# Masked numerators of the first 18 chunks read the scores in PSUM, with a new order for the first third of the work

## The chip, the cores and the metric

The kernel runs on one core of one Trainium2 chip. The metric is the device time of one execution in microseconds (us), as the median of several runs. Before the change it is 442.39 us, from 3 runs between 442.03 and 442.68 us.

Names of engines, as the profile has them: PE is TensorE (PEld is its weight load), DVE is VectorE, ACT is ScalarE, POOL is GpSimd, SP is SyncE, which here only issues DMAs.

## The reference, cut to what matters

Attention with a threshold, for 8 batches of 8 heads with 576 rows and 64 columns each, and then a feed-forward layer with a maximum of three products:

```python
scores = scale * np.matmul(q, k.transpose(0, 1, 3, 2))
thresh = np.max(scores, axis=-1, keepdims=True) - tau
scores = np.where(scores >= thresh, scores, -1000000000.0)
scores = scores - np.max(scores, axis=-1, keepdims=True)
attn = np.exp(scores)
attn = attn / (np.sum(attn, axis=-1, keepdims=True) + 1e-09)
attn_out = np.matmul(attn, v)
...
h = np.maximum(np.maximum(x @ w1, x @ w2), x @ w3)
return h @ w_out
```

Here x is attn_out with heads and columns side by side: 4608 rows of 512. A row keeps only the scores within tau = 0.02 of its largest one; the others become zero in the softmax.

## The kernel before, in words

**Tiles.** The heads of a batch come in two groups of four, called quads (16 quads, g = 0 to 15). A quad has 9 chunks (idx), and a chunk has two tiles (r = 0 and 1). A tile is 128 rows of queries by 576 keys in float32, made by `scores` (line 286) in one of four PSUM slots, s0 to s3, of two banks each (`bank`, line 182). There are 144 chunks and 288 tiles. The first 18 chunks are batch 0, quads 0 and 1.

**The path of one tile.** `maximum` (line 318) reads the scores on DVE and gives a statistic of each row for the bias of the next step: the negated maximum for a masked tile, the maximum less tau for a plain one. `exponents` (line 330) runs on ACT. `numerators` (line 338) gives the numerators of the softmax and their sum. Each tile goes one of two ways, by a digit of the string MASKED (line 24, two digits to a chunk; `masked`, line 310):

- Digit 1, a masked tile. `maximum` writes the negated scores to the SBUF tile z, and its accumulator gives their minimum. After that the PSUM slot is free. `exponents` takes Exp of z in place. `numerators` on DVE (letter k) multiplies z by the test z >= exp(-tau).
- Digit 0, a plain tile. `maximum` writes a bfloat16 tile `unused` that nobody reads, for the accumulator alone. `exponents` reads the scores in PSUM with Prelu, which writes z; then the slot is free. `numerators` on ACT (letter n) takes Exp of z with a factor that sends what lies below the threshold to zero. It issues a second, short ACT instruction that reads the accumulator.

In the first 18 chunks (g < 2) the numerators go straight to P in bfloat16, and their sums are applied later to the product with v (`spread`, line 356, letters R, D, b). For the other chunks they stay in z, and DVE's `reciprocals` (letter r) and POOL's `normalized` (letter p) make P. Then `turned` (line 381, letter t) issues a DMA transpose of the chunk's P on SP.

**After the tiles.** `product` (line 387) multiplies the transposed P with v (letter O, with N for the ninth chunk), and DVE or ACT takes the result out (w and x). `ffn` (line 461) runs the three hidden products (F and B) of a batch, with their evacuation on ACT (h) and DVE (v), and the output products (u, stores o). The hidden products of batch 0 need all four products of quads 0 and 1, so they need all 18 transposes.

**The order.** Every engine works strictly in order: the class `_Ordered` (line 82) ties each instruction to the one before it on its engine. The order of all of them is the string ORDER (line 40), read letter by letter by the loop at line 757 and `issue` (line 634). A digit behind S, T, O, F or D is the PSUM slot that it uses. The letters by engine:

- PE: S scores, T transposes of q and k (`transposed`, line 255), O, N, F, B, D
- DVE: m maximum, k masked numerators, c copy of k, v, w, r, R
- ACT: e exponents, n plain numerators, a copy of q, b, h, x, u
- POOL: q, p, y, z
- SP: l loads of q, k, v (`load`, line 186), g weight loads, t transposes, o stores

All instructions go through one helper, so the profile puts them all down to L91; a tile's name tells them apart (sc: scores in PSUM, z, P, nm: the negated maximum, ptq: the transposed P, o: product, xt: its copy in SBUF, ph: hidden product, tp: transposed q or k). The counts of letters that matter: up to the first F, the order has 49 S, 11 T, 50 m, 49 e, 26 n, 22 k and 27 l.

Of the kernel before, what the change touches and what calls it, by code (L numbers as in the profile page):

```python
# [39 lines left out]
ORDER = """  # L40
mleS2lllgllnlllmS3mmS1lmleT0eS3eT2S1knmcamS0S2mekkeT3tS0eaS1T3mqS2qmgqmnneyzmeyeekleS0tS1mltlnS2S0ketcnmzS3n
meyqmS1mgkemeS2mneS3S0S1mneeT3tkenmmkaT2S1lkletcS3ttemltS0nmeS2emlnekmqS1mktlT3S2S0mRnamteS3genmleeS1S0teS2T
3kmmyS0qelS1qknntecmS3ymmqetS0menneS2meS3S0mS2T1nammtkkmD3D1ebeO3ktbkkenenekO1NwS0wS3rmrS1mmlneeeT2pncS3S0T2
mtplS1RmS3ratpzpzpmlmS2ltqD0eeknD3bbeO0gO3krklpmenpNyelprS1gwwmntS0F2T3mqppeBqcS0S1mmhnzF3F2ezBkevBS0remnnpq
F1tT3BvaheS0klF2S3BmprmppqS1evF0mreneS2gBF3mvngS1keBphF0rrmF2neBS3pvtmBptF1zppS0vzpnBttnS2eT3thmrmT0ectS1aen
mF0S3kreBmnevS2S1gF0S3mgpmnetpeBppqF2rmS1qqplteBvnmT0zrcF3S1hpzmS2plBnS0O1mnentvO3NeemkrF2ekS0rwxmS3nF1pmngB
pyplplgvetBS0rehnS2lmF3S1pBlmF2rtmepevneS0lpzzBS3ptmS1vS0nF2mmenretS1kmnerppepS3mmBepuyuS0kF3S1S2ttenmT0rppk
emanBurmpqS1ppS0ukkmemreO2eO3NS1qllltexllntklpltS0wtmF2F3meBT1eBlprkhncrF0T2laT1vcBS3F2pS1vBynF0mmnrekhqqeS3
mBprvF2nS1pBmpF0enpS3BevS1yS2yphpS0tpmemS3mmF2teF1emtBteBkovetrF0vlnllT3T2BpakT1qpchS3llaS0mtmF1nS2nBreF0peS
3BpmvrmeF1nvS2eBF0nrhmpS3BepkS1pymnS2pltlqnerlO3pvqpmO0eNrmkqwT1explS2F0S3cBmnS1nrmS3vtepmmF2eneF0pBkrnyppS3  # L50
hS1BletomtmnF2T3ByavvrotS1mS0oemF3ppkeF2eekrkuS1T0T3npapnBS3cmrpS0muupS1eS2lmttmmqeeekF0S3rkeS1npppmrtnT2Bcm
S3S2O1nuemuekmkrO0pqNlpewteS3S2qpprtxltltF1lpoqnpnmS0BmeS2hF3emmeeF1BnS0BkrvmnrF2loS3BvpleyyrS1mnpmpphS0ppF3
etmS2emllBeF0nF1BtevkrpS3BvS2nS0hmmtleS1lmmetF2tkF3eBpleT0BvrvanT1nF2cS0BnmF3S1BrhkF2mpeT0vnrBpprveaS3S1nmT0
S2pqpncmpS3meeeqmeS0tO1pqmtotlloeO2ltqNF3S0klwBxrpkppS1mrhmF2S3epBmF1nenS0pvBF3mF2nleBBtottvkS1hF3keF0rurvpm
T2BeapkppyrpvS0S1mnS2S3pnemF0mtS2emkS1rpBenepltS3memkmrutpuS1neS2emF0rmpqkynpS1pqeBemS3uuS1O2kmemekO0NeS3rwT
1xoF0olppnT2mnT3BcS1aS2rncqhF3qtF0pBtemmpBkevrF1eS2vlmpnBptnlS3S0S2hermmempS1F3ypmF0BBelrteoevnF2T1F3akkqvBB
S1nhkymF0pqpnF2verBBS3rvtpmhnS1S0F2mrmlpBpeS3evlmS1eF0pnS2BmnleF1mtllvrlttS3eppptyBmS0ehF2lepT1BmltnS3lnltcS
0rkvO1O2tmNpmeprT0nnexrapkwS3pqF2qyemT0T1cpBF3S0anepkBS1hvF2S3mreBF0mekmrnvF1qBeS2vS3unpS1tS0omlrmeppqptlmmn
F2pktT3BpecS0eekryuT1uaS3mnS2lomtmrtleF1enpS0kpS2qppnemmS3BmkerppeueqS0S3mnurO2kmO0NkwxT3S1eeS0cmpmF2F3kkeBB
hF1eF2pvrBS0nnBvpttS3hmemS1mrppF0rpS2BeenmeF3S1vBF0nkvmS2mlnBS3otolhF1llterlmF0kBlpypvpBtvteeprS2F3rT1BpS0nn  # L60
rmpmaS1mtpheS3S2emnF1eT0T3amecBS2ttoS3evyymmS0ppeO1mpqneO2NenqxF3kktF0wBT1lolrlklBpS2vphS3cmnF0mtlteS1nqrtBm
rpF3vrpqpF2lekBeBpnhF0S1vmT3tlpBS2lS1avmpF3tF0mBrnelekS2evutppmrS1qppS0nS3nmF2mrmS0peekenpS1BemmeS3rkS0emuS1
tlT3ueT2mcknrannpepF0S3mS2qppBmtotlmlttkrrpeueS3qqmS2lO1ueemoeO3opptpkklNwS0lS2xF1mS3BnemehF0kT2mrcnpBS3F1rv
S2BltlpnmF0nepmeveS3pkmBS1httnF2eF0mBrBekF3nS1vrBprvpypppS2nmhemeS0S3F2pF1mmBeBrT0eS3kvnapS2vF0nS1mnBrmmreS2
F3pheS0meeBqpnS1mvmeypS0tpS2etlO3qO1mNpmT2neytF0xtlkkrtnweS1ppT3cramBF2S3BnehvppmeS0rF1qqmT2BF3ncveT2ktnBF1v
S0mrnarBhppS3lF2T1qppeBmcS3S0ovmF1mneT2naepBvS3S2enF1mkmrkqpqueenF0nS1tmS3T2cpqBeupurrS2mmottoS1pS3mttneelot
pmS0O2mkkO3rNwrpeexpneF1nkpS3S2S0mBemS3euuppmF0erkS2tltlBptmrF1S3lhtpmeyppBeS0mvO3O2NenmxpS1S0kF3mxemrS2kBF0
enF1vBermF3tBhpyppyektBvS0pmF2F1vBkS0BF3nmehS2vrBmtpO1eotpnevO0NkF3S2krmnrpxpxBhF1S0eBF3mS2F0BnvpmBrS1vS2S3e
hemmF0kppmnF1rBvkBF2F3BF0ehBtkvevoF2pptkttO1O3NuprBwS2xS3vmmpeS1ekF0S2pmF3oeBmrBokettF1peuokoruoF2uhF0pkkF1h
vvruF2pF0F1hppF3pvvF2F0vvF1F3F2hvtovhtF0F1F3F2htvF0voF1O3uvO2NvF0xwF1hF2F3vF1vhF2F3F1hvF2vvF3F1F2vF3hF1hovF2  # L70
vF3F1vhF2vvF3vBuuF1BuouoF2uooo
"""


# [723 lines left out]
```

## Time and profile before

| what | us |
|---|---|
| median of 3 runs (lowest, highest) | 442.39 (442.03, 442.68) |
| the profiled execution's own time | 442.07 |
| its span, first to last instruction | 440.3 |
| PE busy in the span | 421.6 |
| DVE busy | 400.6 |
| ACT busy | 386.1 |
| POOL busy | 287.1 |

The mean granted clock of PE was 0.993. Between the span and the execution's own time lie 1.77 us outside the instructions. The busy time of an engine is the union of its instructions, so matmuls that overlap count once. The list of groups gives for each kind of instruction its count, its total busy time and its mean in ns. The view by windows cuts the span into stretches and gives each engine's busy time in each of them, with the count of instructions in brackets. The chain of waits follows the work back from its end, each step to what released it.

### The profile page before, as it was taken

What the parts mean: (1) busy time and instruction counts of PE and PEld (TensorE: products, weight loads), DVE (VectorE), ACT (ScalarE), POOL (GpSimd) and SP (SyncE); (2) the same over time, 40 slices, a digit from 0 to 9 for tenths busy, and PEclk for the clock granted to TensorE, in tenths of its full rate; (3) what the DMA queues carried; (4) which work ended last, traced back from release to release, by engine and by line L of the source; (5) the groups of instructions that cost most, each with busy time, mean ns of one, the idle gap of its engine ahead of it and who ended that gap; (6) DMA issues with size and microseconds to landing.
All of it is one profiled execution on the core that took longest, in us unless ns stands there. A gap on an engine that the chain in (4) does not pass through costs nothing.

```text
span 440.3 us, 14164 instructions
## 1 busy us (share of the span) xinstructions
PE 421.6 (96%) x5273; PEld 307.7 (70%) x5273; DVE 400.6 (91%) x1101; ACT 386.1 (88%) x778; POOL 287.1 (65%) x370
## 2 busy tenths in 40 slices
PE   7768989999999999999999999999999999999995
PEld 5434667767787767877687767877677776777762
DVE  3999999999999999999999999999999999999641
ACT  5999998999999999988999999989999999775422
POOL 3532097889887868586767885678769677554400
PEclk9999999999999999999999999999999999999998
DMA  7999989999999999999899989899989979586803
GB/s 235 315 229 183 246 177 282 212 270 223 217 229 184 249 218 193 189 197 245 189 252 140 254 178 249 155 200 183 243 190 178 238 154 168 82 179 120 177 14 107
DMA packets 212772, 87.43 MB, mean 199 GB/s; under 512 B 185824, under 2 KB 199648, under 8 KB 212704
## 3 DMA queue, kind: packets, MB, share of 16 engines
q1 hardware_dynamic: 212000, 85.69, 93.6%
q8 instruction: 41, 0.67, 0.7%
q10 hardware_dynamic: 704, 0.85, 0.6%
q14 instruction: 27, 0.22, 0.2%
HBM read 34.60 MB, written 9.44 MB: 100 GB/s over the span
## 4 chain that ended last, share of the span: by engine, by line
PE 74%; DVE 8%; ACT 6%; DMA 5%; issue 3%; POOL 2%; SPq 1%; DVEq 0%; POOLq 0%; ACTq 0%
PE ph L91 29%; PE sc L91 25%; PE po L91 10%; PE o L91 7%; ACT z L91 4%; PE tp L91 3%; DVE unused L91 3%; DMA ptq<-P 3%; DVE P L91 2%; DVE z L91 2%; SPq L91 1%; DMA qm<-in_q_dram 1%; POOL P L91 1%; DMA km<-in_k_dram 1%; DVE kt L91 1%
## 5 line engine op out<-in xcount | busy, mean ns | idle before, releaser
L91 POOL TENSOR_SCALAR P<-z,rs 128x576 bf16<-128x576 f32 x252 | 203.1, 819 | 90.2 <-ACT z L91 34.2
L91 PE MATMUL sc<-kt,qt 64*128 64x320 f32 (+2 forms) x640 | 179.4, 424 | 4.2 <-DVE z L91 1.5
L91 PE MATMUL sc<-kt,qs 64*128 64x256 f32 (+2 forms) x640 | 178.0, 413 | 3.9 <-ACT z L91 1.7
L91 PE MATMUL ph<-xt,w 64*128 64x288 bf16 (+2 forms) x2160 | 170.7, 283 | 0.6 <-DVE hm L91 0.3
L91 PEld LDWEIGHTS <-w 64*128 64x128 bf16 (+1 forms) x2160 | 125.2, 94 | 34.2 <-issue 7.7
L91 DVE TENSOR_SCALAR_CACHE_REDUCE unused<-sc 128x576 bf16<-128x576 f32 x169 | 124.5, 749 | 4.6 <-PE sc L91 3.9
L91 ACT ACTIVATE z<-sc,nm 128x576 f32<-128x576 f32 x169 | 121.7, 739 | 6.2 <-DVE unused L91 4.1
L91 PEld LDWEIGHTS sc<-kt,qs 64*128 64x128 f32 (+1 forms) x640 | 91.3, 177 | 23.1 <-ACT z L91 5.0
L91 PEld LDWEIGHTS sc<-kt,qt 64*128 64x128 f32 (+1 forms) x640 | 90.8, 177 | 18.1 <-ACT z L91 4.1
L91 ACT ACTIVATE z<-z 128x576 f32<-128x576 f32 x149 | 100.9, 681 | 0.3
L91 ACT ACTIVATE z<-z,nm 128x576 f32<-128x576 f32 x119 | 90.4, 772 | 4.5 <-DVE z L91 4.4
L91 DVE TENSOR_SCALAR_CACHE_REDUCE z<-sc 128x576 f32<-128x576 f32 x119 | 88.3, 750 | 5.8 <-PE sc L91 3.2
L91 DVE SCALAR_TENSOR_TENSOR z<-z 128x576 f32<-128x576 f32 x103 | 82.3, 811 | 0.3
L91 POOL COPY qs<-qt 64x640 f32<-64x640 f32 (+3 forms) x68 | 49.6, 729 | 31.2 <-ACT qt L91 27.9
L91 PE MATMUL po<-wo,hT 64*128 64x512 bf16 (+1 forms) x480 | 53.7, 357 | 0.1
L91 ACT ACTIVATE hm<-ph 128x576 bf16<-128x576 f32 (+2 forms) x54 | 32.1, 594 | 20.3 <-PE ph L91 19.7
L91 DVE TENSOR_TENSOR hm<-ph,hm 128x576 bf16<-128x576 f32 (+2 forms) x54 | 36.9, 684 | 8.2 <-PE ph L91 8.1
L91 PEld LDWEIGHTS <-hT 64*128 64x128 bf16 (+1 forms) x480 | 26.8, 97 | 19.6 <-issue 3.8
L91 DVE TENSOR_TENSOR hT<-ph,hm 128x576 bf16<-128x576 f32 (+2 forms) x54 | 37.2, 688 | 2.5 <-PE ph L91 0.5
L91 PE MATMUL o<-ptq,vb 128*64 128x64 bf16 (+2 forms) x544 | 36.1, 282 | 0.8 <-DMA ptq<-P 0.8
L91 PEld LDWEIGHTS <-vb 128*64 128x64 bf16 x544 | 21.6, 111 | 16.0 <-issue 6.1
L91 ACT ACTIVATION_READ_ACCUMULATOR z<-z 128x1 f32 x149 | 29.6, 198 | 0.0
(40 smaller groups left out, 296.6 us busy)
## 6 DMA issues: line engine op xcount, KB each, us to landing
vm<-in_v_dram SPq DMA_DIRECT2D x32, 256.0 KB, 4.9
out_dram<-ob SPq DMA_DIRECT2D x31, 256.0 KB, 3.3
qm<-in_q_dram SPq DMA_DIRECT2D x15, 512.0 KB, 4.8
km<-in_k_dram SPq DMA_DIRECT2D x15, 512.0 KB, 5.6
stage<-in_moe_w_dram SPq DMA_DIRECT2D x9, 512.0 KB, 5.6
ptq<-P SPq DMA_TRANSPOSE x144, 4.3
stage<-in_moe_w_out_dram SPq DMA_DIRECT2D x3, 512.0 KB, 4.8
qm<-in_q_dram SPq DMA_DIRECT2D x16, 64.0 KB, 2.6
```

Of the source, the lines that this page charges most:

```text
L91: ins = fn(*a, **kw)
```

## The change

A constant DIRECT = 18 is added. A masked tile of the first 18 chunks no longer writes z in `maximum`. Its `maximum` is the form of the plain tile, less tau, whose accumulator gives the threshold (the row's maximum less tau), and a second DVE instruction of 128 by 1 elements negates it for the bias. `exponents` reads the scores in PSUM and writes Exp to z. `numerators` on DVE compares the scores in PSUM with the threshold and multiplies by z. So the PSUM slot of such a tile is free after `numerators` and not after `maximum`.

MASKED changes in its first 36 digits, those of the first 18 chunks: 16 masked tiles become 11. The rest of it stays. ORDER changes in its first 1133 of 2698 letters (a letter and its slot count as one); after that only the slots 0 and 1 change places. No letter's total changes but k (119 to 114) and n (169 to 174). Up to the first F the new order has 49 S, 12 T, 49 m, 49 e, 31 n, 17 k and 27 l.

```diff
 MASKED = """
-001110011000100011010110010010010101111000101101001001000000100000011000
+001001001010010010010010100010010000111000101101001001000000100000011000
...
 PBUFS = 6
+DIRECT = 18
...
 ORDER = """
-mleS2lllgllnlllmS3mmS1lmleT0eS3eT2S1knmcamS0S2mekkeT3tS0eaS1T3mqS2qmgqmnneyzmeyeekleS0tS1mltlnS2S0ketcnmzS3n
-meyqmS1mgkemeS2mneS3S0S1mneeT3tkenmmkaT2S1lkletcS3ttemltS0nmeS2emlnekmqS1mktlT3S2S0mRnamteS3genmleeS1S0teS2T
-3kmmyS0qelS1qknntecmS3ymmqetS0menneS2meS3S0mS2T1nammtkkmD3D1ebeO3ktbkkenenekO1NwS0wS3rmrS1mmlneeeT2pncS3S0T2
-mtplS1RmS3ratpzpzpmlmS2ltqD0eeknD3bbeO0gO3krklpmenpNyelprS1gwwmntS0F2T3mqppeBqcS0S1mmhnzF3F2ezBkevBS0remnnpq
+mS2elmelllgnlmS3lS0mgllmezS2eT3keT1nS0lmaeS3tcnS1mknlmeT2teqyqmateS0S2nqnkS3mzqS1mlmeT0etemS2cnmekS0S1nmemyn
+keS3meeS0gmkS2nenS1melmltS3emkT0alnS2enlmtqT0cS1S3mlnmS0emektntS2eeS1S3lmltnmeekmS2T0S1tnlmmetageS3S0nknmS2l
+emqeymeT1cS3enS1kmtnS2myeRqyqemneS0mS3S1mS0T3emS2nD1ttankmmD3lbebekO1enlllkettO3nNwS0wS1rS2nlmmteeT3S1rpmS0c
+RpzpeT3mpnzamerntS2pS1S3mqD0mkkrekbeneD1lmrbeptO0glgO2NS1S3twT0nwF2mpBcemhS0ppS1F3kzqyemneF2BrmeBtvS0qnpF3T1
...
+    def direct(c, r):
+        return c["n"] < DIRECT and masked(c["g"], c["idx"], r)
+
...
     def maximum(c, r):
 
         nm = small.tile([128, 1], F32, name="nm")
-        if masked(c["g"], c["idx"], r):
+        if direct(c, r):
+            unused = small.tile([128, S], BF16, name="unused", bufs=2)
+            c["t", r] = small.tile([128, 1], F32, name="thr")
+            vector.tensor_scalar(out=unused, in0=c[r], scalar1=tau, scalar2=None,
+                                 op0=OP.subtract, op1=OP.max, accum_out=c["t", r])
+            vector.tensor_scalar(out=nm, in0=c["t", r], scalar1=-1.0, scalar2=None, op0=OP.mult)
+        elif masked(c["g"], c["idx"], r):
             vector.tensor_scalar(out=z_of(c, r), in0=c[r], scalar1=-1.0, scalar2=None,
                                  op0=OP.mult, op1=OP.min, accum_out=nm)
...
     def exponents(c, r):
 
         zn = z_of(c, r)
-        if masked(c["g"], c["idx"], r):
+        if direct(c, r):
+            scalar.activation(out=zn, in_=c[r], func=AF.Exp, bias=c["bias", r], scale=1.0)
+        elif masked(c["g"], c["idx"], r):
             scalar.activation(out=zn, in_=zn, func=AF.Exp, bias=c["bias", r], scale=-1.0)
...
-        if masked(g, idx, r):
+        if direct(c, r):
+            vector.scalar_tensor_tensor(out=to, in0=c[r], scalar=c["t", r], in1=zn,
+                                        op0=OP.is_ge, op1=OP.mult, accum_out=acc)
+        elif masked(g, idx, r):
             vector.scalar_tensor_tensor(out=to, in0=zn, scalar=thr, in1=zn,
                                         op0=OP.is_ge, op1=OP.mult, accum_out=acc)
```

More of the change, by code (lines that the diff above doesn't have):

```diff
@@ L24 @@
 MASKED = """
-001110011000100011010110010010010101111000101101001001000000100000011000
+001001010001010010010010100010010000111000101101001001000000100000011000
 001010100111100001001001000100010001011100101001100010001010010000111000
@@ L40 @@
 ORDER = """
-mleS2lllgllnlllmS3mmS1lmleT0eS3eT2S1knmcamS0S2mekkeT3tS0eaS1T3mqS2qmgqmnneyzmeyeekleS0tS1mltlnS2S0ketcnmzS3n
-meyqmS1mgkemeS2mneS3S0S1mneeT3tkenmmkaT2S1lkletcS3ttemltS0nmeS2emlnekmqS1mktlT3S2S0mRnamteS3genmleeS1S0teS2T
-3kmmyS0qelS1qknntecmS3ymmqetS0menneS2meS3S0mS2T1nammtkkmD3D1ebeO3ktbkkenenekO1NwS0wS3rmrS1mmlneeeT2pncS3S0T2
-mtplS1RmS3ratpzpzpmlmS2ltqD0eeknD3bbeO0gO3krklpmenpNyelprS1gwwmntS0F2T3mqppeBqcS0S1mmhnzF3F2ezBkevBS0remnnpq
-F1tT3BvaheS0klF2S3BmprmppqS1evF0mreneS2gBF3mvngS1keBphF0rrmF2neBS3pvtmBptF1zppS0vzpnBttnS2eT3thmrmT0ectS1aen
@@ L46 @@
[L46 to L70, printed above, removed]
@@ L71 @@
-vF3F1vhF2vvF3vBuuF1BuouoF2uooo
+mS2elmelllgnlmS3lS0mgllmezS2eT3keT1nS0lmaeS3tcnS1mknlmeT2teqyqmateS0S2nqnkS3mzqS1mlmeT0etemS2cnmekS0S1nmemyn
+keS3meeS0gmkS2nenS1melmltS3emkT0alnS2enlmtqT0cS1S3mlnmS0emektntS2eeS1S3lmltnmeekmS2T0S1tnlmmetageS3S0nknmS2l
+emqeymeT1cS3enS1kmtnS2myeRqyqemneS0mS3S1mS0T3emS2nD1ttankmmD3lbebekO1enlllkettO3nNwS0wS1rS2nlmmteeT3S1rpmS0c
+RpzpeT3mpnzamerntS2pS1S3mqD0mkkrekbeneD1lmrbeptO0glgO2NS1S3twT0nwF2mpBcemhS0ppS1F3kzqyemneF2BrmeBtvS0qnpF3T1
+rzpBqvlS2nmaqF0kS1mgpgehetBtS3rmvnmtepF2eS0mBF1pnS3evBF2pF0hBS1krmrBpnveF3S2pznpmvpBnmetS0T1rmchnT2aS3mezpeS
@@ new lines @@
+2pekrmF1nBS0S3evrmF1S2tnmmpeBeF0S3lpgqepqppBgT2vmnrzpzF1thS3ctmS0BnnS2O3pqtmeeneltvmkO1gNrepF0S2xngkS1nrwltm
+emF3BBvpplS2rympS0ehnF1tS3elBF2tpztlmznmlpS0BvremtepvS1nmS3enpmrkS0F2epmrnetS3pS1BemmeS0ukpypmuS1eF3S2rnpT0l
+tBepkanmkrS1llS0qmtkO2uuppO3memeeNeS1lklS0rwlltxpF2mmlpnqeF3rkBT1ehBF0T2ncT1aBvcvpS3yyqqF2S1mmnrneBkhF0S3mep
+BF2S1pnvpernmBltF0epS3vBrS1hmpmS2eS0lmemS3F2ppmyF1eekeBvBF0nlT3aT2ltrBltopnvptrT1qS3ckhamneS2F0mS1BemF2pvrpe
+S3mlnpBeF0pS1vBqF2tqtotS3ltmBkrpnhennmS0S1evrlppmO3ryeO2qplmppkNeT0S1xF2tlltwcnmS3BS0nnrmeS3eF1nvmF2eBmS3hS0
@@ new lines @@
+penpylrtkmpmrBF1T3BvvtoeS0aS2pypeF3memuenkF1kkqpS0T3T2nartmBeppS0rcuultmS2ypeS3ompmS1S2F0eetmklenrS3pkmrmT1B
+S2cnS3O1neuuemkpepO0NpqmetkrS2wpqtxpnS3mnemF0S1BS3mrrmqF2eBkhpeF0S1BovpnteF2S3pmlnrlveBnhlS0tlmppmlS1rellF3t
+lltppmS2emByvF1peneF0BnkvrS3BppS2mtmS1hS0F2mmeF3BkeeeT1atBnnvtorT0vF2cS1BnmF3S0BrhkF2mpeT1vnrBpprveaS3S0nmT1
+S2pqpncmpS3meeeqmeS1tO0pqmtotlloeO2ltqNF3S1klwBxrpkppS0mrhmF2S3epBmF0nenS1pvBF3mF2nleBBtottvkS0hF3keF1rurvpm
+T2BeapkppyrpvS1S0mnS2S3pnemF1mtS2emkS0rpBenepltS3memkmrutpuS0neS2emF1rmpqkynpS0pqeBemS3uuS0O2kmemekO1NeS3rwT
@@ new lines @@
+0xoF1olppnT2mnT3BcS0aS2rncqhF3qtF1pBtemmpBkevrF0eS2vlmpnBptnlS3S1S2hermmempS0F3ypmF1BBelrteoevnF2T0F3akkqvBB
+S0nhkymF1pqpnF2verBBS3rvtpmhnS0S1F2mrmlpBpeS3evlmS0eF1pnS2BmnleF0mtllvrlttS3eppptyBmS1ehF2lepT0BmltnS3lnltcS
+1rkvO0O2tmNpmeprT1nnexrapkwS3pqF2qyemT1T0cpBF3S1anepkBS0hvF2S3mreBF1mekmrnvF0qBeS2vS3unpS0tS1omlrmeppqptlmmn
+F2pktT3BpecS1eekryuT0uaS3mnS2lomtmrtleF0enpS1kpS2qppnemmS3BmkerppeueqS1S3mnurO2kmO1NkwxT3S0eeS1cmpmF2F3kkeBB
+hF0eF2pvrBS1nnBvpttS3hmemS0mrppF1rpS2BeenmeF3S0vBF1nkvmS2mlnBS3otolhF0llterlmF1kBlpypvpBtvteeprS2F3rT0BpS1nn
@@ new lines @@
+rmpmaS0mtpheS3S2emnF0eT1T3amecBS2ttoS3evyymmS1ppeO0mpqneO2NenqxF3kktF1wBT0lolrlklBpS2vphS3cmnF1mtlteS0nqrtBm
+rpF3vrpqpF2lekBeBpnhF1S0vmT3tlpBS2lS0avmpF3tF1mBrnelekS2evutppmrS0qppS1nS3nmF2mrmS1peekenpS0BemmeS3rkS1emuS0
+tlT3ueT2mcknrannpepF1S3mS2qppBmtotlmlttkrrpeueS3qqmS2lO0ueemoeO3opptpkklNwS1lS2xF0mS3BnemehF1kT2mrcnpBS3F0rv
+S2BltlpnmF1nepmeveS3pkmBS0httnF2eF1mBrBekF3nS0vrBprvpypppS2nmhemeS1S3F2pF0mmBeBrT1eS3kvnapS2vF1nS0mnBrmmreS2
+F3pheS1meeBqpnS0mvmeypS1tpS2etlO3qO0mNpmT2neytF1xtlkkrtnweS0ppT3cramBF2S3BnehvppmeS1rF0qqmT2BF3ncveT2ktnBF0v
@@ new lines @@
+S1mrnarBhppS3lF2T0qppeBmcS3S1ovmF0mneT2naepBvS3S2enF0mkmrkqpqueenF1nS0tmS3T2cpqBeupurrS2mmottoS0pS3mttneelot
+pmS1O2mkkO3rNwrpeexpneF0nkpS3S2S1mBemS3euuppmF1erkS2tltlBptmrF0S3lhtpmeyppBeS1mvO3O2NenmxpS0S1kF3mxemrS2kBF1
+enF0vBermF3tBhpyppyektBvS1pmF2F0vBkS1BF3nmehS2vrBmtpO0eotpnevO1NkF3S2krmnrpxpxBhF0S1eBF3mS2F1BnvpmBrS0vS2S3e
+hemmF1kppmnF0rBvkBF2F3BF1ehBtkvevoF2pptkttO0O3NuprBwS2xS3vmmpeS0ekF1S2pmF3oeBmrBokettF0peuokoruoF2uhF1pkkF0h
+vvruF2pF1F0hppF3pvvF2F1vvF0F3F2hvtovhtF1F0F3F2htvF1voF0O3uvO2NvF1xwF0hF2F3vF0vhF2F3F0hvF2vvF3F0F2vF3hF0hovF2
@@ L72 @@
+vF3F0vhF2vvF3vBuuF0BuouoF2uooo
 """
```

## The prediction

> **What bounds the kernel now.** I read the page first, then the busy time by stages, then the chain of waits where one stage gives way to the next.
>
> ```profile
> span 440.3 us, 14164 instructions
> PE 421.6 (96%) x5273; PEld 307.7 (70%) x5273; DVE 400.6 (91%) x1101; ACT 386.1 (88%) x778; POOL 287.1 (65%) x370
> ```
>
> PE is the bound over the whole. The stages show where its missing 18.7 us lie. The columns of the windows are the stretch, its length, then busy us of PE, PEld, DVE, ACT and POOL, with counts in brackets, then the granted clock, the DMA share and GB/s.
>
> ```profile
> 0.00:8.50 8.50, 6.44 (x61) 5.28 (x61) 1.82 (x5) 3.06 (x7) 1.88 (x9) 1.00 0.74 224
> ...
> 185.00:430.00 245.00, 244.67 (x3154) 181.80 (x3151) 226.43 (x624) 210.30 (x425) 165.42 (x208) 1.00 0.90 181
> ```
> ```profile
> 8.50:67.00 58.50, 47.66 (x481) 30.00 (x483) 56.41 (x157) 55.74 (x112) 26.14 (x35) 0.97 1.05 234
> 67.00:75.00 8.00, 8.00 (x117) 6.61 (x115) 7.53 (x19) 7.11 (x14) 5.84 (x8) 1.00 1.11 256
> 75.00:185.00 110.00, 109.10 (x1419) 81.52 (x1417) 106.94 (x297) 107.59 (x218) 87.77 (x113) 1.00 1.08 221
> ```
>
> From 67 to 430 us PE idles 0.00 + 0.90 + 0.33 = 1.2 us, so there is next to nothing to win there. From 8.5 to 67 it idles 58.50 - 47.66 = 10.8 us. In that stretch DVE idles 2.1 us and ACT 2.8 us: both together are the bound of this first stage, which holds the 18 chunks of batch 0. What ends it is read from the chain of waits (start, us, what):
>
> ```profile
> 55.35 3.00 ACT z L91 x6
> 58.35 4.45 DMA ptq<-P
> 62.80 0.14 issue
> 62.94 2.57 PE o L91 x24
> ...
> 65.56 0.77 DVE xt L91
> ...
> 67.18 0.43 PE ph L91 x8
> ```
>
> The eighteenth transpose leaves at 58.35 and lands 4.45 us later, then come the product, its copy xt, and the hidden products (ph). From there PE always has work. So the change moves the end by as much as it moves this point, less the PE work that it puts ahead of it, plus whatever idle time it makes behind it.
>
> **The change part by part.** On an engine that is always busy, what counts is the distance from one start to the next:
>
> ```profile
> 11.99 0.67 ACT L91 ACTIVATE P<-z 128x576 bf16<-128x576 f32 x1
> 12.57 0.19 ACT L91 ACTIVATION_READ_ACCUMULATOR P<-z 128x1 f32 x1
> 12.66 0.69 ACT L91 ACTIVATE qt<-tp 128x640 f32<-128x640 f32 x1
> ```
> ```profile
> 11.55 0.75 DVE L91 SCALAR_TENSOR_TENSOR P<-z 128x576 bf16<-128x576 f32 x1
> 12.23 0.08 DVE L91 DVE_READ_ACCUMULATOR P<-z 128x1 f32 x1
> ```
>
> A plain numerator takes 12.66 - 11.99 = 0.67 us of ACT. A masked one takes 12.23 - 11.55 = 0.68 us of DVE, since the accumulator's read lies beside the next instruction. The change turns five masked tiles into plain ones (k 119 to 114, n 169 to 174). That is +5 x 0.67 = +3.35 us on ACT and -5 x 0.68 = -3.40 us on DVE.
>
> The operations that change their source stand beside their nearest rows:
>
> ```profile
> L91 DVE TENSOR_SCALAR_CACHE_REDUCE unused<-sc 128x576 bf16<-128x576 f32 x169 | 124.5, 749 | 4.6 <-PE sc L91 3.9
> L91 ACT ACTIVATE z<-sc,nm 128x576 f32<-128x576 f32 x169 | 121.7, 739 | 6.2 <-DVE unused L91 4.1
> L91 ACT ACTIVATE z<-z,nm 128x576 f32<-128x576 f32 x119 | 90.4, 772 | 4.5 <-DVE z L91 4.4
> L91 DVE TENSOR_SCALAR_CACHE_REDUCE z<-sc 128x576 f32<-128x576 f32 x119 | 88.3, 750 | 5.8 <-PE sc L91 3.2
> ```
> ```profile
> L91 DVE TENSOR_TENSOR hm<-ph,hm 128x576 bf16<-128x576 f32 x42 | 31.4, 748 | 0.8 <-PE ph L91 0.8
> ```
> ```profile
> L91 DVE SCALAR_TENSOR_TENSOR P<-z x16: 747/750/1568, 11.6 to 50.9; 128x576 bf16<-128x576 f32 x16
> ```
>
> - The maximum of a masked tile writes bfloat16 and not float32: 749 against 750 ns. Giving up the copy in SBUF saves nothing by itself.
> - All 16 once masked tiles now have their exponents read from PSUM. Exp from PSUM is not in the trace. Its bounds are Prelu from PSUM (739) and Exp from SBUF (772); I take the first, for the source is the same: -16 x 0.033 = -0.5 us on ACT, 0 at the other end.
> - The masked product gets one input in PSUM and one in SBUF. The nearest row with two such inputs is hm<-ph,hm at 748 ns, against a median of 750 for the form of today. I take 0. The other end: one of the 16 took 1568 ns, so up to 0.8 us could go. [...]
> - Eleven negations of 128 by 1 are new on DVE, each behind the accumulator that it reads. The nearest rows are a reciprocal behind its own accumulator, and a product behind its own input:
>
> ```profile
> 79.77 0.08 DVE L91 DVE_READ_ACCUMULATOR z<-z 128x1 f32 x1
> 79.88 0.23 DVE L91 RECIPROCAL rs<-sm 128x2 f32<-128x2 f32 x2
> 80.02 0.74 DVE L91 TENSOR_SCALAR_CACHE_REDUCE unused<-sc 128x576 bf16<-128x576 f32 x1
> ```
> ```profile
> 409.91 0.42 DVE L91 TENSOR_TENSOR hm<-ph,hm 128x256 bf16<-128x256 f32 x1 [0.79 <-PE ph L91]
> 410.44 0.42 DVE L91 TENSOR_TENSOR hT<-ph,hm 128x256 bf16<-128x256 f32 x1
> ```
>
> The reciprocal starts 0.11 us behind the start of the read, and two of them take 0.14 us, 0.07 each. So a negation costs 0.07 if nothing waits, 0.18 by the reciprocal, and 0.26 by the product, which starts 0.11 behind the end of what it reads (0.08 + 0.11 + 0.07). I take 0.18, the same kind of dependency: 11 x 0.18 = +2.0 us on DVE, with 0.8 and 2.9 as the ends. Behind a negation that waits stands the next maximum or product on DVE; the tile's own exponents on ACT come as much later.
>
> The sum is 3.35 - 0.5 = +2.8 us on ACT and -3.4 + 2.0 = -1.4 us on DVE (-3.4 to -0.5), both of it ahead of the first hidden product. ACT would need 55.74 + 2.8 = 58.5 us of the 58.5 in the stage. It can't fill every gap, so ACT is the bound there. What its idle time can take up:
>
> ```profile
> 66.09 0.19 ACT L91 ACTIVATION_READ_ACCUMULATOR z<-z 128x1 f32 x1
> 67.75 0.74 ACT L91 ACTIVATE z<-sc,nm 128x576 f32<-128x576 f32 x1 [1.47 <-DVE unused L91]
> ```
>
> The last gap, 1.47 us, comes since the maximum it waits for stands behind xt on DVE. Late work of ACT can lie in it. That leaves 2.8 - 1.47 = 1.35 us. Of the 8.00 - 7.11 = 0.9 us that ACT idles from 67 to 75 I let half go, 0.45 us, since those gaps come in small pieces. Left is 0.9 us. Against it stands PE work: the new order has one transposition more ahead of the first hidden product (12 T against 11), and ten matmuls of it take 0.57 us:
>
> ```profile
> 55.58 0.57 PE L91 MATMUL tp<-identf,km 64*128 64x64 f32 x10
> ```
>
> So 0.9 - 0.5 = **+0.4 us**. The transposes hide ACT's lateness before the eighteenth one:
>
> ```profile
> 55.76 1.32 SPq L91 DMA_TRANSPOSE ptq<-P  x1
> 57.19 0.62 SPq L91 DMA_DIRECT2D vr<-in_v_dram  x1
> 58.35 1.30 SPq L91 DMA_TRANSPOSE ptq<-P  x1
> ```
> ```profile
> 53.05 0.20 ACT L91 ACTIVATION_READ_ACCUMULATOR P<-z 128x1 f32 x1
> ```
>
> The last numerators of batch 0 end at 53.25, but their transpose leaves at 58.35, behind others on SP. So 2.8 us on ACT cost nothing at that place. But two more loads stand ahead of it in the new order (25 l against 23); at 0.62 us each they put it off by 1.2 us if SP never waits otherwise (the weight loads ahead of it are as many, 4). SP's queue and ACT's would then be late by about the same, side by side, so I don't add them.
>
> The profiled execution took 442.07 us, the median is 442.39. 442.07 + 0.4 = 442.5 for a profiled one; for the median 442.39 + 0.4 = **442.8 us**.
>
> **The rivals.**
>
> *ACT's surplus stays whole (slower).* Place: ACT from 8.5 to 67 us. If it idles there as long as before, because the exponents of a masked tile now wait for a second DVE instruction, all 2.8 us come through, less 0.5: +2.3, 444.7 us. It decides from about 1.4 us of ACT idle time in that stage on. For it: the two engines have 1.4 us more work together, where they are the bound. Against it: DVE gets lighter, and ACT's gaps were waits for DVE.
>
> *Slots held too long (slower).* Eleven tiles keep their PSUM slot through exponents and product, 0.6 + 0.7 + 0.2 = 1.5 us longer each at least, and the next scores wait:
>
> ```profile
> PEld sc L91 <- ACT z L91: 5.4, 7, 1.4
> ```
>
> From 10 to 60 us scores already waited seven times for a slot that ACT held, 0.8 us each. If each of the 11 puts DVE off by 0.3 us beyond its 1.4 us of relief, that is 11 x 0.3 - 1.4 = +1.9, 444.3 us. Against it: PE idles 10.8 us there.
>
> *The transposes leave sooner (faster).* The eighteenth waited 5.1 us behind its data. With its data 2.8 us later, at 56.05, and no queue, it would leave 2.3 us sooner than today. If ACT's copies for the sums keep up half that way, the hidden products start 1 to 1.2 us sooner; with the transposition's 0.5, that is -1.5, 440.9 us. [...] Against it: ACT has no time left for it.
>
> **How the numbers follow.** About as before, by ACT's surplus half absorbed: 0.40. ACT's surplus whole: 0.22. Slots: 0.14. Sooner transposes: 0.24. A measurement of this kernel can tell some 0.2%, 0.9 us, from no change. That gives faster 0.24, same 0.40, slower 0.36. The forecast's own range is 441.5 to 443.3. The range of 8 in 10 reaches to both outer cases with the ends of the unknown costs: upward 444.7 + 0.5 = 445.2, if the exponents save nothing, and downward 440.9 - 0.4 = 440.5, if half of the 0.8 us of the long product is won as well. Some 0.1 is left out on each side.
>
> **What would show it.** In the profile after: ACT's busy time from 8.5 to 67 at 57 us or more and DVE's below 56; 11 small instructions on DVE, each 0.18 us ahead of the next; the exponents at 739 and the masked products at 750 ns; the first hidden product between 66.5 and 68 us; PE idle time behind 75 us still near 1.2. I am wrong if the first hidden product comes before 66 or behind 69 us, if a masked product from PSUM takes more than 800 ns, or if PE idles more than 2 us between 75 and 185 us.

## The result, and the profile after

The kernel after takes 444.81 us, the median of 20 runs (442.74 to 446.56), beside 442.69 us for the kernel before in 20 runs on the same chip. The ratio is **1.0036** with a 95% interval of 1.0020 to 1.0052, so it is slower by some 1.6 us (the two medians lie 2.1 us apart). The forecast was 442.8 us and "about as before"; the time lies in the range of 440.5 to 445.2, but it came out as the slower case.

Single runs of one kernel spread over 4 to 5 us here, and the profiled execution of the kernel after is one of its quickest: 442.87 us. Its page begins:

```profile
span 441.1 us, 14189 instructions
...
PE 422.7 (96%) x5273; PEld 307.6 (70%) x5273; DVE 398.2 (90%) x1102; ACT 388.7 (88%) x788; POOL 285.1 (65%) x370
```

The stages of the kernel after, in the columns of the prediction (stretch, length, busy us of PE, PEld, DVE, ACT and POOL, granted clock, DMA share, GB/s):

```profile
8.50:67.00 58.50, 47.12 (x473) 30.23 (x473) 53.53 (x155) 57.04 (x119) 22.28 (x32) 0.94 1.08 234
67.00:75.00 8.00, 7.81 (x98) 5.68 (x100) 7.64 (x21) 6.63 (x13) 7.44 (x10) 1.00 1.15 306
75.00:185.00 110.00, 109.78 (x1418) 81.10 (x1415) 106.06 (x296) 108.06 (x221) 88.08 (x113) 1.00 1.10 217
185.00:430.00 245.00, 244.90 (x3174) 182.22 (x3171) 227.22 (x627) 211.29 (x426) 165.43 (x208) 1.00 0.93 181
```

From 75 us on PE idles 0.3 us, less than before. All of the loss lies ahead of it. The first hidden product now starts at 68.9 us instead of 66.9. So the fair stretch to compare is the one up to that product. Before, then after:

```profile
8.50:66.90 58.40, 47.56 (x480) 29.91 (x482) 56.31 (x157) 55.74 (x112) 26.05 (x35) 0.97 1.05 234
```
```profile
8.50:68.90 60.40, 48.90 (x488) 31.39 (x489) 55.10 (x158) 58.55 (x122) 24.18 (x34) 0.94 1.08 238
```

ACT has 58.55 - 55.74 = **+2.8 us** of work up to that point, DVE 55.10 - 56.31 = -1.2 us. The stretch is 2.0 us longer. ACT's idle time fell from 58.40 - 55.74 = 2.7 to 60.40 - 58.55 = 1.85 us, so 0.8 us of its surplus was absorbed and 2.0 us came through. DVE's idle time rose from 2.1 to 5.3 us. That busy and idle time add up to the longer stretch holds for every engine; who is late, the chain of waits has to tell.

From 14 to 45 us the engine that it runs through has changed. The shares of the chain by line, before and then after:

```profile
by line: DVE unused L91 30.4%; DVE P L91 24.6%; issue 23.5%; DVE z L91 14.9%; DVE kt L91 7.6%; DVEq L91 0.5%; DVE scales L91 0.5%
```
```profile
by line: ACT z L92 31.5%; ACT P L92 22.1%; issue 17.8%; PE sc L92 12.2%; DVE unused L92 9.6%; ACT qt L92 3.8%; DVE P L92 1.8%; PE tp L92 1.4%; DVE nm L92 1.1%; ACTq L92 0.3%
```

Before, DVE's instructions are 78% of it and ACT's none; after, ACT's are 57% and DVE's 13%. DVE's copies xt of the first products start at 56.1 us instead of 53.6, so the kernel after is already behind there.

What ends the stage is read from the chain of waits of the kernel after (start, us, what):

```profile
59.65 0.75 DVE kt L92
60.40 0.04 issue
60.44 0.46 PE tp L92 x8
60.90 1.59 PE sc L92 x10
...
66.36 0.68 DVE unused L92 x2
67.04 0.09 DVE rs L92
67.13 0.01 issue
67.13 0.75 ACT z L92
...
68.98 0.62 PE ph L92 x8
```

No DMA is in it: before, the eighteenth transpose stood here with 4.45 us. Now the chain changes between DVE, PE and ACT. Where PE waits shows who is late. The first is the kernel after from 8.5 to 69 us, the second the kernel before from 8.5 to 67 (us in total, times, longest):

```profile
PE sc L92 <- ACT z L92: 6.1, 11, 1.1
...
PE sc L92 <- DVE P L92: 1.0, 2, 0.9
...
PE sc L92 <- DVE z L92: 0.5, 1, 0.5
```
```profile
PE sc L91 <- DVE z L91: 2.9, 6, 0.8
PE sc L91 <- ACT z L91: 2.5, 4, 1.0
```

Scores wait for a slot that ACT's exponents still read 6.1 us in all, where it was 2.5 us, and the masked product adds 1.0 us of a new wait; the 2.9 us for DVE's copy of the scores are down to 0.5.

The new operations on DVE, as groups and in one place of the timeline:

```profile
L92 DVE SCALAR_TENSOR_TENSOR P<-sc,thr,z 128x576 bf16<-128x576 f32 x11 | 8.9, 813 | 0.7 <-ACT z L92 0.7
...
L92 DVE TENSOR_SCALAR nm<-thr 128x1 f32<-128x1 f32 x11 | 1.7, 154 | 0.4
```
```profile
22.44 0.08 DVE L92 DVE_READ_ACCUMULATOR unused<-sc 128x1 f32 x1
22.56 0.15 DVE L92 TENSOR_SCALAR nm<-thr 128x1 f32<-128x1 f32 x1
22.63 0.81 DVE L92 SCALAR_TENSOR_TENSOR P<-sc,thr,z 128x576 bf16<-128x576 f32 x1
23.36 0.08 DVE L92 DVE_READ_ACCUMULATOR P<-sc,thr,z 128x1 f32 x1
```

The negation takes 22.63 - 22.44 = 0.19 us from the accumulator's read to the next start. The masked product takes 813 ns on average (807 to 819), against a median of 750 before, and from start to start 23.36 - 22.63 = 0.73 us.

### The profile page after: what moved, and what is told of

Read it like the earlier page. It is cut to its first block, busy times and chain, and to the rows that moved or that the text cites. A ratio compares the mean times of both kernels' runs of the same rounds, so it can differ in the third digit from the quotient of the medians.

```text
span 441.1 us, 14189 instructions
## 1 busy us (share of the span) xinstructions
PE 422.7 (96%) x5273; PEld 307.6 (70%) x5273; DVE 398.2 (90%) x1102; ACT 388.7 (88%) x788; POOL 285.1 (65%) x370
## 4 chain that ended last, share of the span: by engine, by line
PE 85%; ACT 7%; DVE 4%; issue 2%; DMA 1%; POOL 0%; SPq 0%; ACTq 0%; POOLq 0%
PE ph L92 32%; PE sc L92 29%; PE po L92 11%; PE o L92 9%; ACT z L92 4%; PE tp L92 4%; ACT P L92 2%; DVE unused L92 1%; DVE z L92 1%; ACT qt L92 1%; PE warm L92 1%; DMA out_dram<-ob 1%; PE d L92 0%; DVE xt L92 0%; DVE kt L92 0%
## 5 line engine op out<-in xcount | busy, mean ns | idle before, releaser
L92 PE MATMUL sc<-kt,qs 64*128 64x256 f32 (+2 forms) x640 | 180.2, 416 | 4.3 <-ACT z L92 1.8
L92 DVE TENSOR_SCALAR_CACHE_REDUCE unused<-sc 128x576 bf16<-128x576 f32 x185 | 136.1, 750 | 6.1 <-PE sc L92 4.9
L92 ACT ACTIVATE z<-sc,nm 128x576 f32<-128x576 f32 x185 | 133.1, 741 | 6.3 <-DVE unused L92 2.9
L92 PEld LDWEIGHTS sc<-kt,qs 64*128 64x128 f32 (+1 forms) x640 | 92.4, 178 | 22.1 <-ACT z L92 4.9
L92 PEld LDWEIGHTS sc<-kt,qt 64*128 64x128 f32 (+1 forms) x640 | 91.8, 178 | 21.5 <-ACT z L92 9.5
L92 ACT ACTIVATE z<-z,nm 128x576 f32<-128x576 f32 x103 | 78.2, 771 | 4.2 <-DVE z L92 4.1
L92 DVE TENSOR_SCALAR_CACHE_REDUCE z<-sc 128x576 f32<-128x576 f32 x103 | 76.4, 751 | 5.4 <-PE sc L92 3.6
L92 POOL COPY qs<-qt 64x640 f32<-64x640 f32 (+3 forms) x68 | 48.3, 710 | 35.3 <-ACT qt L92 31.8
```

The lines of the kernel that those rows point to most:

```text
L92: ins = fn(*a, **kw)
```

## The experiments

**Theory 1, ACT's surplus:** five more plain numerators give ACT more than its gaps can take, and the rest shows at the first hidden product. **Theory 2, the new order's hand-offs:** the engines wait for one another at other places, whatever the loads are. Beside them stand the new form itself (negation, slower product, slots held longer) and SP's queue with its loads and transposes.

In this table "rest" is the profiled run's time less the start of its first hidden product. It is 374 to 377.6 us for kernels that differ by 11 us: what moves that product moves the end. But each row stands for one execution, and "rest" itself differs by 1.2 us between before and after, so a difference of 1 to 2 us in one row proves little without the ratio. The profiled runs of e8, e12 and e13 are the slowest of their kernels and that of e9 is 1.9 us above its median; in e8's, PE idles 1.8 us between 67.1 and 80 us, hence its 377.6. "Idle" is the length from 8.5 us to the first hidden product less the busy time. The last column is the issue of the eighteenth transpose and its landing.

| kernel | ratio to before (95%) | median | profiled | first product | rest | ACT busy, idle | DVE busy, idle | 18th transpose |
|---|---|---|---|---|---|---|---|---|
| before | 1 | 442.69 | 442.07 | 66.9 | 375.2 | 55.7, 2.7 | 56.3, 2.1 | 58.4, 62.8 |
| after | 1.0036 (1.0020, 1.0052) | 444.81 | 442.87 | 68.9 | 374.0 | 58.6, 1.9 | 55.1, 5.3 | 59.5, 62.4 |
| e1 | 1.0055 (1.0026, 1.0085) | 444.93 | 445.61 | 69.9 | 375.7 | 58.7, 2.7 | 53.8, 7.6 | 60.9, 65.3 |
| e2 | 1.0087 (1.0064, 1.0111) | 446.08 | 444.86 | 69.3 | 375.6 | 58.5, 2.3 | 53.8, 7.0 | 57.3, 60.3 |
| e3 | 1.0050 (1.0028, 1.0071) | 444.38 | 444.63 | 69.5 | 375.1 | 56.7, 4.3 | 57.1, 3.9 | 59.7, 62.6 |
| e4 | 1.0085 (1.0062, 1.0108) | 445.69 | 446.47 | 71.3 | 375.2 | 57.7, 5.1 | 58.5, 4.4 | 59.6, 62.7 |
| e5 | 1.0061 (1.0040, 1.0082) | 444.73 | 444.36 | 68.8 | 375.6 | 59.2, 1.1 | 56.7, 3.7 | 58.2, 61.1 |
| e6 | 1.0081 (1.0049, 1.0113) | 445.38 | 444.79 | 69.6 | 375.2 | 56.6, 4.5 | 55.2, 5.9 | 60.9, 65.5 |
| e7 | 1.0024 (1.0005, 1.0043) | 443.45 | 443.62 | 68.5 | 375.1 | 56.3, 3.7 | 59.1, 0.9 | 57.6, 60.5 |
| e8 | 0.9996 (0.9972, 1.0020) | 442.07 | 444.71 | 67.1 | 377.6 | 56.0, 2.7 | 56.4, 2.2 | 57.8, 60.7 |
| e9 | 1.0056 (1.0032, 1.0079) | 445.26 | 447.17 | 71.8 | 375.4 | 56.3, 7.0 | 56.5, 6.8 | 62.8, 67.7 |
| e10 | 1.0089 (1.0062, 1.0116) | 445.84 | 446.88 | 71.1 | 375.8 | 61.8, 0.8 | 55.6, 7.0 | 61.7, 64.6 |
| e12 | 1.0210 (1.0179, 1.0241) | 451.62 | 453.25 | 77.9 | 375.4 | 56.6, 12.8 | 58.0, 11.4 | 65.3, 70.1 |
| e13 | 1.0102 (1.0074, 1.0130) | 446.44 | 448.63 | 71.7 | 376.9 | 59.2, 4.0 | 58.2, 5.1 | 62.7, 65.6 |

The kernel before ran beside each group with medians of 442.06 (e1 to e4), 441.96 (e5 to e8) and 442.58 us (the others).

### e1: the new order and masks without the new form

```diff
-DIRECT = 18
+DIRECT = 0
```

> The new masks (11 masked tiles) and the new order, but with the old form of a masked tile: its maximum copies the scores to SBUF, no negation, and the PSUM slot is free after the maximum. Theory 'ACT surplus' (five more plain tiles make ACT late, and with it the first hidden product): ACT's work hardly changes (11 exponents from SBUF again, +0.3 us), so the first hidden product stays at 68.5 to 69.5 us and the ratio to before at 1.003 to 1.005. Rival 'form' (negations, slower products and held slots make the loss): DVE sheds 11 x 0.24 = 2.7 us and the slots are free sooner, first hidden product at 66.9 to 67.5, ratio 0.999 to 1.001. Rival 'loads' (two more loads on SP ahead of the eighteenth transpose): no change, 68.9.

The ratio is 1.0055, with an interval that overlaps that of the kernel after. DVE has 55.1 - 53.8 = 1.3 us less work up to the first hidden product, and nothing comes of it. **The loss is in the order and the masks; the form adds nothing that these runs can tell.** The chain of waits of e1 shows a second thing:

```profile
60.93 4.42 DMA ptq<-P
65.34 0.04 issue
65.39 2.57 PE o L92 x24
...
69.06 0.76 DVE xt L92
69.82 0.04 issue
69.86 0.68 PE ph L92 x8
```

Here the stage ends through the eighteenth transpose, as before the change, but 2.6 us later on SP (60.93 against 58.35).

### e2: the old order and form, four masked tiles made plain

```diff
-001110011000100011010110010010010101111000101101...
+001110011000100001010100010000010100111000101101...
 ORDER: the k of tiles (8,0), (11,0), (14,0) and (17,1) becomes n at its place
```

> The kernel before, its order and its form, but with four of the 16 masked tiles of the first 18 chunks made plain, each numerator at its old place in the order, on ACT and no longer on DVE. Theory 'ACT surplus': ACT gets 4 x 0.67 = 2.7 us more, DVE 2.7 less; first hidden product at 68 to 69.3 us (66.9 before), ratio to before 1.002 to 1.005. Rivals 'form' and 'loads': neither the form nor the loads are touched, so 66.9 and 0.999 to 1.001.

Four tiles moved to ACT in the old order cost 1.0087, more than the whole change and more than theory 1 allowed (1.005): some 3.8 us (2.8 to 4.9 by its interval of 1.0064 to 1.0111), against 2.8 us of added work. The place of the work in the order may count beside its amount; no run separates the two. ACT gets +2.8 us up to the first hidden product, as in the kernel after, and it comes 2.4 us later:

```profile
8.50:69.30 60.80, 47.38 (x483) 30.34 (x482) 53.82 (x150) 58.50 (x121) 25.06 (x34) 0.97 1.07 242
```

The marks of the kernel after are here too, without its order and form: from 14 to 45 us ACT's instructions are 66% of the chain of waits, and up to 69 us the scores wait 7.8 us for ACT's exponents (2.5 before, 6.1 in the kernel after).

### e3 and e4: the new order, with tiles made masked again

```diff
-001001010001010010010010100010010000111000...
+001001011001010110010110101010011000111000...
-DIRECT = 18
+DIRECT = 0
 ORDER: the n of tiles (4,0), (7,1), (10,1), (13,0) and (16,0) becomes k at its place (e3)
 e4: DIRECT stays 18, only (4,0), (7,1) and (10,1) become masked
```

> The new order with the old form of a masked tile, and five of its plain tiles made masked at the same places in the order: 16 masked tiles as before. Theory 'ACT surplus': ACT sheds 3.35 us against the changed kernel; first hidden product at 66 to 67.3 us, ratio to before 0.997 to 1.001. Rival 'form': as with 11 masked tiles in the old form, within 0.3 us. Rival 'loads': 68.9 us and 1.003 as in the changed kernel.

> The changed kernel with its new form, and three plain tiles made masked at the same places in the order: 14 masked tiles. Theory 'ACT surplus': ACT sheds 3 x 0.67 = 2.0 us, DVE takes on 3 x 0.92 = 2.8 us, of which it had 5 us idle; first hidden product at 66.9 to 68 us, ratio to before 0.999 to 1.002. Rival 'form': three more negations and three more held slots, first hidden product at 69 to 69.8, ratio 1.004 to 1.006. Rival 'loads': 68.9 us.

In e3 both engines have nearly their loads of before (ACT 1.0 us more, DVE 0.8), and the end does not come back:

```profile
8.50:69.50 61.00, 48.12 (x491) 31.33 (x490) 57.07 (x158) 56.73 (x114) 26.23 (x34) 0.94 1.04 235
```
```profile
ACT z L92 <- DVE unused L92: 2.9, 4, 1.0
```

ACT has 1.8 us less work than in the kernel after and idles 4.3 us, 2.9 of them for DVE's maxima, a wait that came in through the moved tiles. So theory 1 misses, but the edit changed the hand-offs as well: DVE's instructions are back to 32% of the chain from 14 to 45 us, beside ACT's 40%. e4 is slower still, beyond all that was expected (71.3 us, 1.0085); nothing of it separates the theories, since it adds work to DVE (58.45 us).

### e5 and e7: the old order, with work added to ACT alone or DVE alone

```diff
 exponents(c, r)
+if n in (8, 14, 20, 26, 32):
+    scalar.activation(out=spare, in_=z_of(c, r), func=AF.Exp, scale=-1.0, accum_out=acc)
```
```diff
 if masked(c["g"], c["idx"], r):
+    if (c["n"], r) in MORE:
+        vector.tensor_scalar(out=spare, in0=c[r][:, 0:160], scalar1=-1.0, scalar2=None, op0=OP.mult)
```

> The kernel before, with nothing of the change but a load on ScalarE of the size that the change brings: behind the exponents number 9, 15, 21, 27 and 33 one more exponential of 128x576 of the z tile, with its accumulator, whose result nobody reads (about 0.67 us each, 3.35 us together). Theory 1 (ScalarE's surplus sets the first hidden product): the first hidden product leaves 1 to 2 us later, at 68 to 69, the ratio is 1.002 to 1.005. Theory 2 (the new order itself, with its hand-offs, is late, and ScalarE has room): the first hidden product stays at 66.9 +- 0.4 and the ratio within 1.001 of 1.

> The kernel before, with what the new form adds to VectorE and nothing else: ahead of eleven of the masked maxima one more instruction of 128x160 from PSUM (about 0.24 us, the 0.18 of the negation and the 0.06 by which the masked product from PSUM turned out longer; 2.65 us together). Theory 1 (VectorE was as full as ScalarE before, and what is added to either shows): the first hidden product is 1 to 2.5 us later, the ratio 1.002 to 1.005. Theory 2 (VectorE has room and the form is free in any order): within 0.4 us of 66.9 and within 1.001 of 1.

e5, then e7:

```profile
8.50:68.80 60.30, 47.24 (x481) 30.10 (x483) 56.65 (x157) 59.17 (x122) 25.21 (x34) 0.97 1.04 234
```
```profile
8.50:68.50 60.00, 49.88 (x482) 32.73 (x483) 59.07 (x168) 56.33 (x112) 26.17 (x34) 0.91 1.04 246
```

ACT with 59.17 - 55.74 = 3.4 us more is 1.9 us later (ratio 1.0061, a little over what theory 1 gave). DVE with 59.07 - 56.31 = 2.8 us more is 1.6 us later (1.0024). In these profiles each added us costs 0.55 to 0.6 us on either engine; by the ratios it is some 0.8 on ACT and 0.4 on DVE. From 14 to 45 us ACT's instructions are 82% of the chain in e5, DVE's 65% in e7. That answers to theory 1 in the old order, where both engines were full, and **what ACT's load alone does is shown here**: it is enough for a loss of the size of the change.

### e6 and e9: the new order, with work taken from ACT

```diff
+elif (c["n"], r) in ((3, 0), (6, 0), (10, 0), (13, 0), (16, 0)):
+    pool.tensor_copy(out=to, in_=zn)
+    pool.memset(acc, 1.0)
```
```diff
+elif (c["n"], r) in SHORT:
+    vector.memset(to[:, 64:S], 0.0)
+    scalar.activation(out=to[:, 0:64], in_=zn[:, 0:64], func=AF.Exp, scale=-1.0, accum_out=acc)
```

> The kernel after, with five of its plain numerators, (3,0), (6,0), (10,0), (13,0) and (16,0), taken off ScalarE: GpSimd copies z to the tile instead and sets the row sum to one, so that the second exponential of these five tiles is left out. ScalarE does 3.35 us less in the new order, all else stands. Theory 1 (ScalarE's surplus): the first hidden product comes back to 66.5 to 67.5, the ratio against the kernel before is 0.998 to 1.001. Theory 2 (the new order itself is late): the first hidden product stays at 68.5 to 69.5 and the ratio at 1.003 to 1.005.

> The kernel after, with seven of its plain numerators, (3,0), (6,0), (8,1), (10,0), (12,1), (14,1) and (16,0), done for the first 64 columns only; VectorE sets the other 512 to zero just ahead, in an instruction that waits for no result. Left out is the numerator of these columns. ScalarE gets about 3.3 us less (seven times some 0.47), VectorE up to 1.5 us more, so that both stand near their loads of the kernel before, in the new order and without GpSimd's queue, which muddled the earlier try. Theory 1 (ScalarE's surplus): the first hidden product at 66.5 to 67.8, the ratio at 0.998 to 1.0015. Theory 2 (the new order's hand-offs are late by themselves): 68.5 to 69.5, 1.003 to 1.005.

Both miss what theory 1 expected, and both lie above theory 2's range as well: 1.0081 and 1.0056, first hidden product at 69.6 and 71.8 us. ACT has about 2 us less work than in the kernel after and idles 4.5 and 7.0 us. The chain of waits says what is late in its place, e6 first:

```profile
60.94 4.55 DMA ptq<-P
65.49 0.04 issue
65.53 2.51 PE o L92 x24
```
```profile
45.06 7.89 DMA ptq<-P
...
62.78 4.88 DMA ptq<-P
67.66 0.04 issue
67.70 2.51 PE o L93 x24
```

The eighteenth transpose leaves 1.4 and 3.3 us later than in the kernel after (59.53) and sets the end. In e9 ACT itself waits for an earlier transpose to release a P tile:

```profile
ACT P L93 <- DMA ptq<-P: 1.8, 2, 1.4
```

From 14 to 45 us ACT's instructions are 44% of the chain in e6, beside 25% for DVE's, and from 44.07 us on the chain stands 7.71 us at a transpose; in e9 they are 48%, beside 30% for DVE's. So the two tell that relief of ACT alone does not bring the time back in this order, and that DVE and the transposes on SP are next. They do not tell what ACT's surplus costs by itself, since another limit took over.

### e8: the old order, with two loads moved behind the eighteenth transpose

```diff
 ORDER: two l leave the place ahead of the eighteenth t ("mmlneee" to "mmneee", "mtplS1R" to "mtpS1R")
        and stand behind it ("S3ratpz" to "S3ratllpz")
```

> The kernel before, with the two loads that stand ahead of the eighteenth transposition on the first third's order moved behind it; nothing else. The change moves two loads the other way, ahead of the eighteenth, and its issue came 1.2 us later. Theory 1 (ScalarE's surplus) and theory 2 (new order's hand-offs) both expect nothing here: first hidden product at 66.9 +- 0.4, ratio within 1.001 of 1. A third theory, that SyncE's queue sets the end of the stage, expects the first hidden product 0.5 to 1.2 us sooner and a ratio of 0.997 to 0.999.

The eighteenth transpose leaves 0.5 us sooner and lands at 60.7 instead of 62.8 us, and nothing comes of it: 0.9996 (0.9972 to 1.0020), the first hidden product at 67.1. Most of the 2.1 us need not be the loads': it landed 2.9 us after its issue instead of 4.45, as in e2, e5 and e7 (2.9 to 3.0), where the loads stand as before. In the old order SP is not the only limit either. The mirror of it, the new order with its loads behind the eighteenth transpose, was not tried.

### e10 and e13: the new order, with work added to ACT alone or DVE alone

The edits are those of e5 (128x540) and e7, made to the kernel after.

> The kernel after, with five more exponentials of 128x540 on ScalarE behind the exponents number 9, 15, 21, 27 and 33, results read by nobody: about 0.64 us each, 3.2 us together, as was done to the kernel before. Theory 1 (ScalarE is the engine that sets the new order's end): nearly all of it comes through, since ScalarE idles less than in the kernel before: the first hidden product 2 to 3.2 us later, at 70.9 to 72.1, ratio against the kernel before 1.007 to 1.011. Theory 2 (hand-offs, ScalarE has room): at most 0.8 us later, ratio under 1.006.

> The kernel after, with eleven more instructions of 128x160 from PSUM on VectorE ahead of the eleven masked maxima, as was done to the kernel before (2.75 us of busy time there). VectorE idles 5.3 us up to the first hidden product in the kernel after. Theory 1 (ScalarE's surplus): VectorE has room, the first hidden product is at most 0.8 us later (under 69.7), ratio 1.003 to 1.005. Theory 2 (every hand-off between the two counts, whichever is fuller): 1 to 2 us later as in the kernel before, ratio 1.006 to 1.009.

```profile
8.50:71.10 62.60, 47.39 (x489) 29.93 (x490) 55.64 (x158) 61.80 (x132) 24.28 (x34) 0.97 1.07 228
```
```profile
8.50:71.70 63.20, 50.29 (x488) 32.22 (x488) 58.15 (x169) 59.23 (x123) 23.91 (x33) 0.89 1.06 218
```
```profile
ACT z L92 <- DVE nm L92: 2.5, 5, 1.0
```

e10 (first row) is as theory 1 had it: 61.80 - 58.55 = 3.25 us more on ACT, the first hidden product 2.2 us later, 1.0089. From 14 to 45 us ACT's instructions are 90% of its chain. e13 (the others) goes the way of theory 2 and beyond its range (1 to 2 us, 1.009): DVE had 5.3 us of idle time, and 3.05 us more on it (58.15 - 55.10) cost 2.8 us, and the ratio rose by 0.0066 where the same edit raised it by 0.0024 in the old order. The wait of ACT for the negated maximum is 2.5 us there, against 1.2 in the kernel after. **Idle time of DVE in the new order is no room:** it sits behind slots and maxima that the others wait for.

### e12: one part alone in the old order, exponents from PSUM

```diff
-    if masked(...):  tensor_scalar(out=z_of(c, r), ..., op0=OP.mult, op1=OP.min, accum_out=nm)
+    if c["n"] < 18 and masked(...):  the same with out=unused
...
-    scalar.activation(out=zn, in_=zn, func=AF.Exp, bias=c["bias", r], scale=-1.0)
+    scalar.activation(out=zn, in_=c[r], func=AF.Exp, bias=c["bias", r], scale=1.0)
```

> The kernel before in its own order and with its own masked tiles, with one part of the change alone: the masked maxima of the first 18 chunks write a tile that nobody reads, with the sign already turned, so that no negation is needed, and the exponents of these 16 tiles come from PSUM; the masked product stays on the two reads in SBUF. ScalarE gets 16 x 0.031 = 0.5 us less, a PSUM slot is held 0.75 us longer in 16 tiles. By theory 1 the first hidden product comes 0 to 0.3 us sooner (66.6 to 66.9), ratio 0.999 to 1.000. By theory 2 the longer hold of the slots delays scores in an order not laid out for it: 0.3 to 1.5 us later, 1.001 to 1.003.

Both theories are far off: 1.0210, the largest loss of all, with no work added. The window, then the waits of PE and ACT:

```profile
8.50:77.90 69.40, 51.14 (x481) 34.71 (x482) 58.02 (x156) 56.64 (x113) 26.25 (x34) 0.90 1.02 212
```
```profile
PE sc L91 <- ACT z L91: 16.5, 14, 2.7
...
ACT z L91 <- DVE unused L91: 8.8, 11, 1.6
DVE unused L91 <- PE sc L91: 8.6, 13, 1.9
```

Sixteen tiles hold their slot through the exponents, the scores wait 16.5 us (up to 72 us) where it was 2.5, and DVE and ACT wait behind them in turn. So holding a slot longer costs 9 us (451.62 against 442.58) in an order that gives the slot away early. The new order is laid out for it: there the form is free (e1). The whole new form in the old order wasn't tried; in that order the next scores of the slot stand ahead of the masked product for 15 of the 16 tiles. What that would do is not shown.

## Why the prediction was right or wrong

1. **The bound.** Right. The stage ahead of the first hidden product sets the time, and what follows it takes 374.0 to 377.6 us in all fourteen kernels. That ACT would become the bound there was right too: the chain of waits went over from DVE to ACT.
2. **ACT +2.8 us.** Right: +2.8 (58.55 against 55.74).
3. **DVE -1.4 us.** Measured -1.2. The parts do not add up to it by themselves: with the slower product they give some -0.6; the sum left out that the new order has one maximum less ahead of the first hidden product (49 m against 50, an estimated 0.7 us by the 749 ns of one). The negation costs 0.19 us (0.18 forecast). The masked product was costed at nothing and takes 813 ns against 750, 63 ns or 11 x 0.06 = 0.7 us in all. I had gone by the row of hm<-ph,hm, another instruction with one input in PSUM, at 748 ns; its time did not carry over, and why the two differ no run shows. My own bound of 800 ns for being wrong was passed here. It did not decide: e1, without the new form, is no faster.
4. **Half of ACT's surplus absorbed: the step that failed.** 1.47 + 0.45 us of ACT's idle time were to take it up, and 0.5 us of PE work to be gained; the first hidden product was to come between 66.5 and 68 us and came at 68.9. ACT's idle time up to the first hidden product shrank by 0.8 us only, so 2.0 us were left and not 0.9. The gap of 1.47 us ran from 66.28 to 67.75 us, across the first hidden product at 66.9: work of ACT in it is already late for what ends the stage. Whether the transposition ahead (8 matmuls more up to that point) gave its 0.5 us back can't be told: "rest" is 1.2 us shorter in this one profile. The result, +1.6 us by the ratio, lies between the forecast (+0.4) and the rival "ACT's surplus stays whole" (+2.3, chance 0.22), nearer to the rival. The time is inside the range because the range reached out to that rival, not because this step was right.
5. **SP's 1.2 us not added.** The eighteenth transpose left 59.53 - 58.35 = 1.2 us later, the amount worked out. That the two loads did it is not shown: in e8 two loads moved its issue by 0.5 us only. But two latenesses side by side mean that the later one counts, and I forecast less than either. In e1, e6 and e9, all in the new order, it leaves another 1.4 to 3.3 us later and ends the stage; in the profiled run of the kernel after it landed at 62.4 and did not. Where it ended the stage (before, e1, e6, e9), it took 4.4 to 4.9 us to land; in the kernel after it took 2.9. What sets the landing time stays open.
6. **Slots.** The rival had the wrong kernel: in the new order the form costs nothing measurable, in the old one (e12) slots held longer cost 9 us.
7. **Transposes sooner (-1.5).** Fell at the place that counts: the first fourteen left 0.3 to 3.6 us sooner, but the last four left 1.2 to 2.4 us later, and the stage needs all eighteen. The further 0.4 us at the range's low end, half of what the one long product of 1568 ns took beyond the others, were an estimate that no run shows as a gain: none of the eleven masked products after was that long (807 to 819 ns), and the first hidden product still came 2.0 us later.

What is shown: the loss lies in the new order with its five more plain tiles, not in the new form; the chain of waits, which ran over DVE, runs mostly over ACT in the kernel after; a load of ACT of that size alone costs at least as much in the old order and moves the chain to ACT as well (e5); added work costs in the new order on both engines (e10, e13). What isn't: in the new order three reliefs of ACT (e3, e6, e9) brought nothing back, each with another limit in its place. How much of the 2.0 us is ACT's load and how much the order's own hand-offs and transposes stays open.

## What to carry to other kernels

Where two engines and a queue were all near full, work added to either engine showed at once (0.55 to 0.6 us for each us in e5 and e7), but work taken off ACT brought nothing back (e3, e6, e9: the first hidden product at 69.5 to 71.8 us, against 68.9): look for the second and third latest chain before you price a relief, and let the later of two latenesses count. Idle time absorbs work only if it lies ahead of the instruction that ends the stage, and even there it did not where others waited for what stood behind it (e13: 5.3 us of idle time on DVE, and 3.05 us more work cost 2.8 us); compare the stretch up to that instruction and not a fixed window. Before an operand is moved to PSUM, count how long the slot is then held, and whether the order of the queues gives it away earlier (e12: 9 us lost).
